# Splitting the first weight loads of a fused feed-forward and linear-attention kernel over three DMA queues

## The chip, the cores and the metric

The kernel runs on one core of one Trainium2 chip. A core has TensorE (matmuls, "PE" in the profile, with "PEld" for the loading of the stationary operand), VectorE ("DVE"), ScalarE ("ACT"), GpSimd ("POOL") and SyncE ("SP"), which only issues DMAs. ScalarE and GpSimd can issue DMAs as well. The metric is the device time of one execution in microseconds (us); lower is better. Of the kernel before, three runs were timed, and one further execution was taken with the hardware profiler.

## The reference

Two branches work on the same input x of 2048 rows by 512 columns, and a gate for each row mixes them:

```
qkv = x @ wqkv                                   # 32 heads of 16
phi(t) = [softmax(t @ w_phi), softmax(-t @ w_phi)]   # per head
o = phi(q) (phi(k)^T v) / (phi(q) (phi(k)^T 1) + 1e-6)
a = o @ wo
b = relu(x @ w1 + b1)^2 @ w2 + b2                # 512 -> 1792 -> 512
g = sigmoid(sum(x * gate_w))                     # one number per row
out = g * a + (1 - g) * b
```

All is float32. The change touches only the first part of branch b: the first product with w1.

## The kernel before

To keep float32 accuracy on TensorE the kernel writes every operand as a high part and a low part of the type fp32r: `hi` is a rounded copy, `lo = src - hi`. A product is then three matmuls, high by high, high by low and low by high. So each piece of data that comes from memory passes through two elementwise operations, one copy (mostly on ScalarE) and one subtraction (on VectorE), before TensorE may use it.

The feed-forward branch cuts the 1792 hidden columns into 14 chunks of 128 (a chunk is called `f` or `fc`) and the 2048 rows into 4 blocks of 512. A hidden chunk of one block, called `u`, is a sum over four slices of 128 of the 512 inputs, numbered k = 0 to 3. The weights of seven chunks are held at a time; the kernel sweeps over the blocks twice. Between these matmuls, a table of slots (`at(slot, step)`) spreads the steps of the attention branch over the time. The order on each engine is that in which the program issues the instructions, apart from those that a scheduler with priorities moves; `tc.issue_after(i)` keeps an instruction behind instruction i on that scheduler's list.

What the change touches is the beginning, `warm_up` and `start`:

- `warm_up` (L457) fills a tile `zeros` on VectorE and lets TensorE do 11 matmuls on it (`idle(11)`, L465), whose results are thrown away.
- `start` (L468) computes the first three chunks (`FIRST = 3`) of block 0 together, slice by slice of the inputs, since then each slice can be used as soon as it is there. For each k it loads `xT[0, :, k, :]` (256 KB, by SyncE's queue, tile `in`) and the weights of the three chunks for this k (192 KB, by ScalarE's queue, tile `row`, L478). It makes `xh`, `xl` from the first and `w1h`, `w1l` from the second, and issues nine matmuls (L501). For k = 0 VectorE makes `w1h` (L488) and ScalarE makes `xh` (L491); for the others ScalarE makes both.
- The order of the nine is: all three chunks' xh·w1h, then all three xl·w1h, then all three xh·w1l. Only for k = 3 they go chunk by chunk, so that the first chunk is finished early and `hidden` (L404) can begin on it: ScalarE applies relu with the bias `b1c`, squares, and the result is split into `hh` and `hl`.
- The fourth chunk's weights (`do_w1(FIRST)`) and the first chunk of w2 go into `row` tiles, too, by SyncE's queue (L104). There are six `row` buffers, and these loads take the last two.
- The bias `b1c` is loaded by GpSimd's queue (L126), between the instructions that GpSimd has at the start anyway: the identity matrix `ident`, the zeroing of `kvb` and the ones in three tiles `vext`.
- `gwb` and `b2b`, copies of the gate weights and of the second bias in all partitions (256 KB each), are loaded by SyncE's queue at the slots 2 and 9 (L704, L705). `gwb` is first used at L257, `b2b` at the end of the first block.

A DMA signals its end on one of a small set of semaphores that the framework hands out in turn, eight for the queues of SyncE and ScalarE together. So the ninth such DMA waits on its engine until the first has landed, the tenth until the second, and so on.

Of the kernel before, what the change touches and what calls it, by code (L numbers as in the profile page):

```python
# [10 lines left out]
AF = mybir.ActivationFunctionType  # L11
# [5 lines left out]
P = 128  # L17
S, D, H, DH, F = 2048, 512, 32, 16, 1792
NK = D // P
# [6 lines left out]
FIRST = 3  # L26
# [9 lines left out]
def tile_gated_mix(ctx: ExitStack, tc: tile.TileContext, xT, xn, wqT, wkT, wphi, wv, wo, w1, b1, w2, b2, gw, out):  # L36
    nc = tc.nc
# [12 lines left out]
    def used(p):  # L50
        banks.remove(p)
        banks.append(p)
# [32 lines left out]
    def load(src, eng=nc.sync):  # L85
        t = stage.tile([P, 512], F32, tag="in", name="in")
        eng.dma_start(t, src)
        return t

    def row():  # L90
        return work.tile([P, D], F32, tag="row", name="row", bufs=6)

    def ffn_tiles(nm, fc):
        return (fpool.tile([P, 512], F32R, tag=nm + "h", name=f"{nm}h{fc}"),
                fpool.tile([P, 512], F32R, tag=nm + "l", name=f"{nm}l{fc}"))

    def by_k(tiles):
        return [tuple(z[:, k * P:(k + 1) * P] for z in tiles) for k in range(NK)]

    def load_ffn(nm, src, fc):  # L100

        if (nm, fc) in (("w1", FIRST), ("w2", 0)):
            t = row()
            nc.sync.dma_start(t, src)  # L104
        else:
            t = load(src)
        hi, lo = ffn_tiles(nm, fc)
        split(t, hi, lo, nc.scalar, nc.vector)
        return hi, lo
# [11 lines left out]
    st, up_w, down_w = {}, {}, {}  # L121
# [1 line left out]
    ident = const.tile([P, P], F32, name="ident")  # L123
    make_identity(nc, ident)
    b1c = const.tile([P, NF], F32, name="b1c")
    nc.gpsimd.dma_start(b1c, b1)  # L126
    gwb = const.tile([P, D], F32, name="gwb")
    b2b = const.tile([P, D], F32, name="b2b")
    gate = const.tile([P, NB * NC], F32, name="gate")
# [36 lines left out]
    def joint_start(loaded):  # L166
        wph, *t = loaded
        two = lambda a: a.rearrange("p (h c) -> p h c", h=2)
        st["W"], st["raw"] = {}, {}
        tmp = work.tile([P, 4 * D], F32, tag="phiT", name="tmp", bufs=1)  # L170
        st["tmp"] = tmp[:, :2 * D], tmp[:, 2 * D:]
        st["slots"] = [work.tile([P, 2 * D], F32R, tag=t, name=f"slot{t}", bufs=1) for t in ("o0", "o1", "ez")]
        for k in (0, 2, 1, 3):
            r = st["tmp"][k // 2] if k % 2 else work.tile([P, 2 * D], F32, tag="e", name=f"raw{k}", bufs=2)
            st["raw"][k] = r
            nc.sync.dma_start(two(r)[:, :, 256:], two(wv[k * P:(k + 1) * P, :]))

    def whole(k):
        wph, *t = st["wT"]
# [224 lines left out]
    def hidden(fc, ps):  # L404
        r = work.tile([P, SB], F32, tag="r", name="r")
        with tc.high_priority(offset=AHEAD):
            st["relu"] = nc.scalar.activation(r, ps, AF.Relu, bias=b1c[:, fc:fc + 1])  # L407
        nc.scalar.activation(r, r, AF.Square)  # L408
        hh = work.tile([P, SB], F32R, tag="hh", name="hh", bufs=LAG + 1)
        hl = work.tile([P, SB], F32R, tag="hl", name="hl", bufs=LAG + 1)  # L410
        st["act"] = split(r, hh, hl, nc.scalar, nc.vector)
        st["dve"] = st["lo"]
        return hh, hl
# [24 lines left out]
    def do_joint(j, piece):  # L438
        if (j, piece) == (0, 0):
            joint_start(st["wT"])  # L440
        with tc.issue_after(st["up"].ins):
            joint(j, piece)
        if (j, piece) == (1, 0):
            banks.remove(ps_b)
# [5 lines left out]
    def do_w1(fc):  # L450
        up_w[fc] = by_k(load_ffn("w1", w1[fc], fc))

    def do_w2(fc):
        down_w[fc] = load_ffn("w2", w2[fc * P:(fc + 1) * P, :], fc)


    def warm_up():  # L457
        z = st["zeros"] = work.tile([P, 512], mybir.dt.bfloat16, tag="r", name="zeros")
        nc.vector.memset(z, 0.0)
        st["warm"] = ps_a.tile([P, 512], F32, tag="s", name="warm")  # L460
        idle(11)

    def idle(n):
        for _ in range(n):
            st["up"] = nc.tensor.matmul(st["warm"], st["zeros"][:, :P], st["zeros"], start=True, stop=True)  # L465


    def start():  # L468
        fs, wide = range(FIRST), FIRST * P
        W = [ffn_tiles("w1", f) for f in fs]  # L470
        ps = [p.tile([P, SB], F32, tag="s", name="u") for p in (ps_e, ps_b, ps_f)]
        xs = st["x", 0] = []
        for f in fs:
            up_w[f] = [tuple(z[:, P * f:P * (f + 1)] for z in W[k]) for k in range(NK - 1)]
            up_w[f].append(tuple(z[:, wide:] for z in W[f]))
        for k in range(NK):
            u, t = load(xT[0, :, k, :]), row()
            nc.scalar.dma_start(t[:, :wide].rearrange("p (f c) -> p f c", f=FIRST),  # L478
                                w1[:FIRST, :, k * P:(k + 1) * P].rearrange("f p c -> p f c"))
            xh, xl = (xpool.tile([P, SB], F32R, tag=g, name=f"{g}0_{k}") for g in ("xh", "xl"))  # L480
            xs.append((xh, xl))
            if k < NK - 1:
                w = [(t[:, :wide], *(z[:, :wide] for z in W[k]))]
            else:
                w = [(t[:, P * f:P * (f + 1)], *(z[:, wide:] for z in W[f])) for f in fs]
            for src, hi, lo in w:
                if k == 0:
                    nc.vector.tensor_copy(hi, src)  # L488
                else:
                    nc.scalar.activation(hi, src, AF.Copy)  # L490
            nc.scalar.activation(xh, u, AF.Copy)  # L491
            low = nc.vector.tensor_tensor(xl, u, xh.bitcast(F32), ALU.subtract)
            with tc.issue_after(low.ins):
                for src, hi, lo in w:
                    nc.vector.tensor_tensor(lo, src, hi.bitcast(F32), ALU.subtract)
            terms = [(f, 0, xh) for f in fs] + [(f, 0, xl) for f in fs] + [(f, 1, xh) for f in fs]
            if k == NK - 1:
                terms.sort(key=lambda x: x[0])
            for f, part_, x in terms:
                with tc.issue_after(st["up"].ins):  # L500
                    st["up"] = nc.tensor.matmul(ps[f], up_w[f][k][part_], x, start=k == 0 and (part_, x) == (0, xh),  # L501
                                                stop=k == NK - 1 and part_ == 1)
        do_w1(FIRST)
        for f in fs:
            hid[f] = hidden(f, ps[f])
            if f == 0:
                st["act0"] = st["act"]
        for p in (ps_e, ps_b, ps_f):
            used(p)
# [191 lines left out]
    def at(slot, f, *a):  # L701
        steps.setdefault(int(2 * slot) / 2, []).append(lambda: f(*a))

    at(2, lambda: nc.sync.dma_start(gwb, gw.partition_broadcast(P)))  # L704
    at(9, lambda: nc.sync.dma_start(b2b, b2.partition_broadcast(P)))  # L705
    for fc in range(LAG + 1, NFH):
        if fc > FIRST:
            at(2 * (fc - LAG) - 2, do_w1_first, fc)
        at(2 * (fc - LAG) - (2 if fc == LAG + 1 else 1), do_w2, fc)
# [50 lines left out]
    hid, last = {}, len(work_list) - 1  # L760
# [5 lines left out]
    def do_up(t, between=lambda: None):  # L766
# [4 lines left out]
        else:  # L771
            between()

    warm_up()
    start()
    with tc.issue_after(st["act0"].ins):
        for fc in range(LAG + 1):
            do_w2(fc)
# [80 lines left out]
```

## Time and profile before

| | |
|---|---|
| runs, us | 513.17, 512.70, 510.85 (median 512.70) |
| the profiled execution, us | 511.04 |
| span of the profile, first to last instruction, us | 509.3 |
| TensorE busy, share of the span | 99% |
| VectorE, ScalarE, GpSimd busy | 79%, 50%, 18% |
| mean granted TensorE clock | 0.999 |

The span is 1.7 us shorter than the execution's time, which also holds what lies before the first and behind the last instruction. The rows of the profile read as follows. A row of the timeline has the start in the span, the time taken (of all instructions that it merges), the engine, the line of the code, the operation and the tiles as output<-input, the count, and in brackets how long the engine was idle before it and what ended this idle time. A letter q behind the engine (SPq, ACTq) marks the issuing of a DMA, which isn't counted as work. A row of the list of groups has the busy time, the mean of one in ns, and the idle time before. A row of the DMA issues has the size, and the median time from the issue to the landing in us. A row of a table by stretches has the stretch, its length, the busy time of PE, PEld, DVE, ACT and POOL with the instructions that began there, the granted clock, the DMA engines' busy share and the GB/s.

### The profile page before, as it was taken

The page shows a single profiled execution, that of the slowest core. Times are in us where ns is not written, and L with a number is a line of the kernel's source. Part 1 is how long each engine was busy: PE and PEld are TensorE (multiplying, and loading weights), DVE is VectorE, ACT ScalarE, POOL GpSimd, SP SyncE. Part 2 cuts the span into 40 slices and gives each one's busy share as a digit, 9 for nine tenths or more (in the row PEclk, how much of TensorE's full clock was granted, in tenths as well). Part 3 has the DMA queues.
Part 4 walks back from the last instruction along what each step waited for, and adds up shares of the span by engine and source line. Part 5 has one row for each costly group of instructions (what it writes and reads, how often), then busy time and mean ns, then how long its engine had stood idle before and what let it go on. Part 6 is the DMA issues. An engine that isn't in the chain of part 4 may idle for free.

```text
span 509.3 us, 9129 instructions
## 1 busy us (share of the span) xinstructions
PE 502.8 (99%) x3421; PEld 408.0 (80%) x3421; DVE 403.5 (79%) x668; ACT 254.8 (50%) x445; POOL 91.0 (18%) x106
## 2 busy tenths in 40 slices
PE   8999999999999999999999999999999999999997
PEld 4888888888788888788888878788787878788775
DVE  3559848888884979796998989897969797897723
ACT  4778645556253565463564744444456354333540
POOL 1001640204320024000012140211222120111200
PEclk9999999999999999999999999999999999999999
DMA  8975696667844478762266131324112231032112
GB/s 256 324 247 186 231 325 194 200 210 226 291 167 142 171 237 288 281 208 83 73 198 228 50 96 40 106 72 143 48 32 85 69 88 47 3 120 68 37 27 83
DMA packets 46628, 76.12 MB, mean 149 GB/s; under 512 B 6776, under 2 KB 23928, under 8 KB 46584
## 3 DMA queue, kind: packets, MB, share of 16 engines
q1 hardware_dynamic: 35544, 41.58, 26.5%
q10 hardware_dynamic: 8224, 24.51, 13.8%
q0 software_dynamic: 2816, 9.45, 5.1%
q8 instruction: 27, 0.44, 0.3%
q14 instruction: 17, 0.14, 0.1%
HBM read 57.68 MB, written 11.54 MB: 136 GB/s over the span
## 4 chain that ended last, share of the span: by engine, by line
PE 93%; DVE 3%; DMA 3%; issue 0%; DVEq 0%; ACT 0%
PE d L77 10%; PE d L78 9%; PE d L79 9%; PE u L77 9%; PE u L78 9%; PE u L79 9%; PE att L79 3%; PE att L78 3%; PE q L78 3%; PE q L77 3%; PE att L77 3%; PE q L79 3%; PE pX L579 3%; PE pX L577 2%; PE pX L578 2%; PE pY L577 2%
## 5 line engine op out<-in xcount | busy, mean ns | idle before, releaser
L407 ACT ACTIVATE r<-u,b1c 128x512 f32<-128x512 f32 x56 | 38.5, 687 | 125.3 <-PE u L79 123.8
L77 PE MATMUL d<-w2h,hh 128*128 128x512 f32 x224 | 87.8, 392 | 0.0
L78 PE MATMUL d<-w2l,hh 128*128 128x512 f32 x224 | 87.3, 390 | 0.0
L79 PE MATMUL d<-w2h,hl 128*128 128x512 f32 x224 | 87.2, 389 | 0.0
L77 PE MATMUL u<-xh,w1h 128*128 128x512 f32 x212 | 83.8, 395 | 0.0
L78 PE MATMUL u<-xl,w1h 128*128 128x512 f32 x212 | 82.6, 390 | 0.0
L79 PE MATMUL u<-xh,w1l 128*128 128x512 f32 x212 | 82.5, 389 | 0.0
L322 POOL TENSOR_TENSOR ez<-e,z 128x512 f32<-128x512 f32 x32 | 42.8, 1358 | 165.9 <-ACT e L294 165.9
L67 DVE TENSOR_TENSOR hl<-r,hh 128x512 fp32r<-128x512 f32 x56 | 37.7, 674 | 23.7 <-ACT hh L64 23.7
L77 PEld LDWEIGHTS d<-w2h,hh 128*128 128x128 f32 x224 | 42.1, 188 | 9.1 <-issue 0.4
L78 PEld LDWEIGHTS d<-w2l,hh 128*128 128x128 f32 x224 | 42.1, 188 | 8.9 <-DVE w2l L67 0.4
L79 PEld LDWEIGHTS d<-w2h,hl 128*128 128x128 f32 x224 | 42.1, 188 | 8.8
L77 PEld LDWEIGHTS u<-xh,w1h 128*128 128x128 f32 x212 | 39.8, 188 | 11.0 <-issue 3.1
L79 PEld LDWEIGHTS u<-xh,w1l 128*128 128x128 f32 x212 | 39.8, 188 | 8.4
L78 PEld LDWEIGHTS u<-xl,w1h 128*128 128x128 f32 x212 | 39.8, 188 | 7.8
L297 DVE TENSOR_REDUCE sm<-e 128x64 f32<-128x1024 f32 x27 | 32.8, 1213 | 11.1 <-ACT e L294 11.1
L294 ACT ACTIVATE e<-e 128x1024 f32<-128x1024 f32 x27 | 28.6, 1059 | 25.0 <-DVE e L292 24.7
L64 ACT ACTIVATE hh<-r 128x512 fp32r<-128x512 f32 x56 | 35.1, 627 | 0.9
L408 ACT ACTIVATE r<-r 128x512 f32<-128x512 f32 x56 | 34.9, 624 | 0.8
L360 ACT ACTIVATE phiT<-tb 32x256 f32<-32x256 f32 x64 | 26.4, 412 | 6.1 <-DVE tb L345 5.1
L329 DVE TENSOR_REDUCE dz<-ez 128x64 f32<-128x1024 f32 x16 | 19.4, 1210 | 11.6 <-POOL ez L322 11.6
L616 ACT ACTIVATE tmp<-pX 128x512 f32<-128x512 f32 x24 | 14.3, 597 | 27.3 <-PE pX L579 27.3
(171 smaller groups left out, 982.2 us busy)
## 6 DMA issues: line engine op xcount, KB each, us to landing
sloto<-wkeep ACTq DMA_DIRECT2D x30, 512.0 KB, 4.2
in<-in_xT SPq DMA_DIRECT2D x44, 256.0 KB, 3.7
slotez<-wkeep ACTq DMA_DIRECT2D x15, 512.0 KB, 4.5
phiT<-tb SPq DMA_DIRECT2D x192, 32.0 KB, 1.9
in<-in_w SPq DMA_DIRECT2D x23, 256.0 KB, 3.3
part<-row POOLq DMA_DIRECT2D x16, 256.0 KB, 5.0
row<-part SPq DMA_DIRECT2D x16, 256.0 KB, 3.1
out<-row SPq DMA_DIRECT2D x15, 256.0 KB, 2.2
```

The lines of the kernel that those rows point to most:

```text
L64: i = nc.scalar.activation(hi, src, AF.Copy)
L67: st["lo"] = elo.tensor_tensor(lo, src, hi.bitcast(F32), ALU.subtract)
L77: nc.tensor.matmul(o, ah[:, sa], bh[:, sb], start=first, stop=False)
L78: nc.tensor.matmul(o, ah[:, sa], bl[:, sb], start=False, stop=False)
L79: return nc.tensor.matmul(o, al[:, sa], bh[:, sb], start=False, stop=last)
L294: nc.scalar.activation(ef, ef, AF.Exp)
L297: nc.vector.tensor_reduce(sm, e3, AX.X, ALU.add)
L322: nc.gpsimd.tensor_tensor(ez[:, hs, :], e3[:, hs, :], zbc[half], ALU.mult)
L360: nc.scalar.activation(dst, src, AF.Copy)
L407: st["relu"] = nc.scalar.activation(r, ps, AF.Relu, bias=b1c[:, fc:fc + 1])
L408: nc.scalar.activation(r, r, AF.Square)
L577: nc.tensor.matmul(ps, h, wh, start=first and j == 0, stop=False, skip_group_check=True)
```

## The change

The four loads of the first weights are distributed anew. ScalarE's queue gets the first chunk's part of k = 0 alone (64 KB), then all of k = 1, then all of k = 3. GpSimd's queue gets the other two chunks' part of k = 0 (128 KB), then all of k = 2. For k = 0, VectorE now copies the rows (`xh`), and ScalarE the weights, in two pieces as they were loaded; the matmuls of k = 0 go chunk by chunk, as those of k = 3 do. For the other k, ScalarE copies the rows first and then the weights. The bias `b1c` moves from GpSimd's queue to SyncE's, behind the four loads of rows; `gwb`, `b2b`, the loads of `wv` and of the w2 chunks are held behind the fourth chunk's load. Two of the 11 matmuls on zeros are dropped.

```
         if (nm, fc) in (("w1", FIRST), ("w2", 0)):
             t = row()
-            nc.sync.dma_start(t, src)
+            st["row"] = nc.sync.dma_start(t, src)
...
     b1c = const.tile([P, NF], F32, name="b1c")
-    nc.gpsimd.dma_start(b1c, b1)
...
-            nc.sync.dma_start(two(r)[:, :, 256:], two(wv[k * P:(k + 1) * P, :]))
+            with tc.issue_after(st["row"].ins):
+                nc.sync.dma_start(two(r)[:, :, 256:], two(wv[k * P:(k + 1) * P, :]))
...
     def do_w2(fc):
-        down_w[fc] = load_ffn("w2", w2[fc * P:(fc + 1) * P, :], fc)
+        with tc.issue_after(st["row"].ins):
+            down_w[fc] = load_ffn("w2", w2[fc * P:(fc + 1) * P, :], fc)
...
-        idle(11)
+        idle(9)
...
+        raw = [(load(xT[0, :, k, :]), row()) for k in range(NK)]
+        for eng, parts in (nc.scalar, ((0, 0, 1), (1, 0, FIRST), (3, 0, FIRST))), (nc.gpsimd, ((0, 1, FIRST), (2, 0, FIRST))):
+            last = None
+            for k, a, b in parts:
+                with tc.issue_after(last.ins) if last else nullcontext():
+                    last = eng.dma_start(raw[k][1][:, a * P:b * P].rearrange("p (f c) -> p f c", f=b - a),
+                                         w1[a:b, :, k * P:(k + 1) * P].rearrange("f p c -> p f c"))
+            if eng is nc.scalar:
+                fetched = last
         for k in range(NK):
-            u, t = load(xT[0, :, k, :]), row()
-            nc.scalar.dma_start(t[:, :wide].rearrange("p (f c) -> p f c", f=FIRST),
-                                w1[:FIRST, :, k * P:(k + 1) * P].rearrange("f p c -> p f c"))
+            u, t = raw[k]
...
-            if k < NK - 1:
+            if k == 0:
+                w = [(t[:, a:b], *(z[:, a:b] for z in W[k])) for a, b in ((0, P), (P, wide))]
+            elif k < NK - 1:
...
-            for src, hi, lo in w:
+            with tc.issue_after(fetched.ins):
                 if k == 0:
-                    nc.vector.tensor_copy(hi, src)
+                    nc.vector.tensor_copy(xh, u)
                 else:
-                    nc.scalar.activation(hi, src, AF.Copy)
-            nc.scalar.activation(xh, u, AF.Copy)
+                    nc.scalar.activation(xh, u, AF.Copy)
+                for src, hi, lo in w:
+                    fetched = nc.scalar.activation(hi, src, AF.Copy)
...
-            if k == NK - 1:
+            if k in (0, NK - 1):
                 terms.sort(key=lambda x: x[0])
...
+        nc.sync.dma_start(b1c, b1)
         do_w1(FIRST)
...
+    def rows_alike(t, src):
+        with tc.issue_after(st["row"].ins):
+            nc.sync.dma_start(t, src.partition_broadcast(P))
+
+    at(2, rows_alike, gwb, gw)
+    at(9, rows_alike, b2b, b2)
```

Three places of the order of instructions are shown. The first is GpSimd's beginning, up to its first DMA of weights; `in_w` and `in_b` are the weights and biases in memory. Before:

```order
masks.py:197 MEMSET ident 128x128
L126 DMA b1c<-in_b 128x14
masks.py:199 ISA
masks.py:199 AFFINE_SELECT ident<-ident 128x128
L132 MEMSET kvb 128x256
L139 MEMSET vext_112 128x32
L139 MEMSET vext_113 128x32
L139 MEMSET vext_114 128x32
```

And with the change:

```order
masks.py:197 MEMSET ident 128x128
L131 MEMSET kvb 128x256
masks.py:199 ISA
masks.py:199 AFFINE_SELECT ident<-ident 128x128
L138 MEMSET vext_111 128x32
L138 MEMSET vext_112 128x32
L138 MEMSET vext_113 128x32
L482 DMA row<-in_w 128x2x128
L482 DMA row<-in_w 128x3x128
```

The bias has left this queue, and the two loads of weights (k = 0's other two chunks, and k = 2) stand behind all seven instructions that GpSimd has there.

The second place is TensorE's first nine matmuls on data, all of k = 0, the number behind `u` telling the chunk. Before, the first seven of them:

```order
L501 MATMUL u_138<-xh0_0_145,w1h0_132 128x512
L501 MATMUL u_139<-xh0_0_145,w1h0_132 128x512
L501 MATMUL u_140<-xh0_0_145,w1h0_132 128x512
L501 MATMUL u_138<-xl0_0_146,w1h0_132 128x512
L501 MATMUL u_139<-xl0_0_146,w1h0_132 128x512
L501 MATMUL u_140<-xl0_0_146,w1h0_132 128x512
L501 MATMUL u_138<-xh0_0_145,w1l0_133 128x512
```

And with the change:

```order
L512 MATMUL u_135<-xh0_0_155,w1h0_129 128x512
L512 MATMUL u_135<-xl0_0_156,w1h0_129 128x512
L512 MATMUL u_135<-xh0_0_155,w1l0_130 128x512
L512 MATMUL u_136<-xh0_0_155,w1h0_129 128x512
L512 MATMUL u_136<-xl0_0_156,w1h0_129 128x512
L512 MATMUL u_136<-xh0_0_155,w1l0_130 128x512
L512 MATMUL u_137<-xh0_0_155,w1h0_129 128x512
L512 MATMUL u_137<-xl0_0_156,w1h0_129 128x512
L512 MATMUL u_137<-xh0_0_155,w1l0_130 128x512
```

The three that need only the first chunk's weights now come first, and the fourth is the first that needs what GpSimd's queue loads.

The third place is SyncE's queue behind the loads of rows, as one piece of the difference (a minus is a row of before, a plus one of the change):

```order
 L87 DMA in<-in_xT 128x512 x4
+L514 DMA b1c<-in_b 128x14
 L104 DMA row<-in_w 128x512 x2
-L704 DMA gwb<-in_gw 128x512
+L87 DMA in<-in_w 128x512
+L786 DMA gwb<-in_gw 128x512
+L145 DMA row<-in_wphi 128x512
 L87 DMA in<-in_w 128x512 x2
-L146 DMA row<-in_wphi 128x512
```

The bias stands in front of the fourth chunk's weights, `gwb` has moved back by one load, and `wphi` forward by two.

More of the change, by code (lines that the diff above doesn't have):

```diff
@@ L702, in at @@
         steps.setdefault(int(2 * slot) / 2, []).append(lambda: f(*a))
-    at(2, lambda: nc.sync.dma_start(gwb, gw.partition_broadcast(P)))
-    at(9, lambda: nc.sync.dma_start(b2b, b2.partition_broadcast(P)))
     for fc in range(LAG + 1, NFH):
```

## The prediction

> **What bounds the kernel now.** I read the page first, then the chain of work that ended last, then the windows, and last the timeline of the first 20 us.
>
> ```profile
> PE 502.8 (99%) x3421; PEld 408.0 (80%) x3421; DVE 403.5 (79%) x668; ACT 254.8 (50%) x445; POOL 91.0 (18%) x106
> PE 93%; DVE 3%; DMA 3%; issue 0%; DVEq 0%; ACT 0%
> 60.00:130.00 70.00, 70.00 (x554) 57.77 (x553) 56.42 (x97) 37.95 (x65) 20.28 (x29) 1.00 0.72 244
> 0.74 5.40 DMA row<-in_w
> 6.16 0.37 DVE w1h L488
> 6.67 8.54 PE u L501 x36
> 15.21 0.23 PE u L77
> 17.93 0.23 PE d L77
> 18.16 0.50 PE d L78
> ```
>
> The first two lines are the page's busy times and the shares of the chain: TensorE is busy for 99% and holds 93% of the chain. The third is the table by stretches for 60 to 130 us, where TensorE works without a gap. The rest is the chain in order of time. So behind the beginning almost nothing but TensorE's own work sets the end, and whatever moves the time at which TensorE has done its first 36 matmuls (L501) moves the end by as much. That time is 15.21. Everything below is about this number. Between 15.21 and 17.93 stand twelve matmuls, 2.72 / 12 = 0.227 us each; 36 of them would be 8.16 us, so that 8.54 holds 0.38 us of waits.
>
> What the first of them waits for is in the timeline:
>
> ```profile
> 1.19 4.87 PE L465 MATMUL warm<-zeros 128*128 128x512 bf16 x11 [1.19 <-DVE zeros L459]
> 4.58 0.15 PEld L465 LDWEIGHTS <-zeros 128*128 128x128 bf16 x1 [0.28 <-issue]
> 5.01 0.15 PEld L465 LDWEIGHTS <-zeros 128*128 128x128 bf16 x1 [0.27 <-issue]
> 5.52 0.63 ACT L491 ACTIVATE xh<-in 128x512 fp32r<-128x512 f32 x1 [1.37 <-DMA in<-in_xT]
> 6.16 0.36 DVE L488 CAST w1h<-row 128x384 fp32r<-128x384 f32 x1 [5.03 <-DMA row<-in_w]
> 6.67 0.93 PE L501 MATMUL u<-xh,w1h 128*128 128x512 f32 x3 [0.60 <-DVE w1h L488]
> ```
>
> The rows of k = 0 have landed by 5.52, where ScalarE starts on them. The weights land at 6.16, 0.64 us later; VectorE copies them in 0.37, and 0.14 after that (6.53 to 6.67) TensorE begins. It has idled since 6.06, the end of the matmuls on zeros. So the weights are late, not the rows, and the most that better weights can bring is bounded by the rows at 5.52.
>
> **The change, part by part.** First the three matmuls that need the first chunk's quarter only.
>
> ```profile
> L488 DVE CAST w1h<-row 128x384 fp32r<-128x384 f32 x1 | 0.4, 359 | 5.0 <-DMA row<-in_w 5.0
> L492 DVE TENSOR_TENSOR xl<-in,xh 128x512 fp32r<-128x512 f32 x4 | 2.8, 690 | 2.0 <-ACT xh L491 2.0
> L495 DVE TENSOR_TENSOR w1l<-row,w1h 128x128 fp32r<-128x128 f32 x3 | 0.7, 284 | 0.0
> L490 ACT ACTIVATE w1h<-row 128x384 fp32r<-128x384 f32 x2 | 1.1, 526 | 2.5 <-DMA row<-in_w 2.5
> L490 ACT ACTIVATE w1h<-row 128x128 fp32r<-128x128 f32 x3 | 0.7, 294 | 0.0
> ```
>
> These are groups with the mean of one in ns. The quarter is a third of the bytes that landed at 6.16, first on its queue, so I take it to be there, and copied in 0.29, before the rows are. VectorE's copy of 512 columns isn't in the trace; it lies between the 0.36 of 384 columns and 0.48 in proportion, and I take 0.45. Then `xh` is there at 5.52 + 0.45 = 5.97 and the first matmul starts at 6.11, against 6.67. But the second needs `xl`: 5.97 + 0.69 + 0.14 = 6.80. The third needs the quarter's `w1l`: 6.66 + 0.28 + 0.14 = 7.08, and ends at 7.31. In the old order all three xh·w1h filled this wait; chunk by chunk they can't. So of 0.56 us of earlier start, TensorE stands at 7.31 with three matmuls done and 33 to go. If nothing waits any more, it is through at 7.31 + 33 x 0.227 = 14.80, **0.41 us earlier** than 15.21. That is the whole gain at hand.
>
> The fourth matmul needs the other two chunks' part of k = 0, which now comes by GpSimd's queue.
>
> ```profile
> 1.31 0.70 POOL L126 DMA_DIRECT2D b1c<-in_b  x1 [0.37 <-issue]
> 2.11 0.30 POOL masks.py:199 TENSOR_SCALAR_AFFINE_SELECT ident<-ident 128x128 f32<-128x128 f32 x1
> 2.34 0.32 POOL L132 MEMSET kvb<- 128x256 f32 x1
> 2.59 0.28 POOL L139 MEMSET vext<- 128x32 f32 x3
> b1c<-in_b POOLq DMA_DIRECT2D x1, 7.0 KB, 6.4
> wkeep<-spare POOLq DMA_DIRECT2D x1, 512.0 KB, 2.9
> q0 software_dynamic: 2, 0.00, 1.0%
> 5.00:5.50 0.50, 0.50 (x3) 0.15 (x1) 0.00 (x0) 0.00 (x0) 0.00 (x0) 1.00 1.07 336
> 5.50:6.00 0.50, 0.50 (x2) 0.00 (x0) 0.00 (x0) 0.48 (x1) 0.00 (x0) 1.00 1.10 371
> ```
>
> GpSimd ended at 2.87, with 0.70 for the bias's DMA and 0.37 of idle time before it. With that gone its work ends near 1.8; with the same 0.37 before a DMA the issue begins at 2.1. The two rows of landing times are the ends for what follows: the bias's 7 KB, the first DMA on this queue, took 6.4 us, the 512 KB of a later one 2.9. The row of q0, GpSimd's queue, is that of the DMA view for 5.0 to 5.5 us: two packets, and none stand in the view of 1.3 to 5.0. So the bias's packets began 3.7 to 4.2 us after its issue at 1.31. The load now is the first on the queue in the same microseconds, so this row is the nearest: packets from 5.8 to 6.3 on. The last two rows have the DMA engines fully busy (1.07, 1.10) at 336 to 371 GB/s; at a third of some 350, 128 KB take 1.1 us. **The landing, T, is then 6.9 to 7.4; I take 7.2.** ScalarE's copy of 256 columns is the mean of its 294 and 526 ns, 0.41, and with 0.14 the fourth matmul starts at 7.75. TensorE is through at 7.75 + 33 x 0.227 = 15.24: +0.03 us. The wait that went (for all weights of k = 0) is replaced by one for two thirds of them, at almost the same place. The two cases meet at T = 7.31 - 0.55 = 6.76; above it each us of T is a us of time, and T = 7.17 is the point of no change.
>
> The ends: with T = 2.1 + 2.9 = 5.0 nothing waits, -0.41. With 2.1 + 6.4 = 8.5 and 1.0 us for the 121 KB more, T = 9.5 and the sum is +2.3.
>
> The other k follow from T. ScalarE goes on with `xh` and `w1h` of k = 1 (0.62 + 0.53) until T + 1.56; TensorE wants them at T + 0.55 + 6 x 0.227 = T + 1.91, so 0.2 us are left. For k = 2 ScalarE ends at T + 2.71 and TensorE arrives at T + 3.95, so GpSimd's second load may land 3.3 us behind the first; it is issued one DMA (0.7) later. k = 3 has moved forward on ScalarE's queue. I cost these at nothing, under cover of TensorE's backlog.
>
> Then SyncE's queue.
>
> ```profile
> in<-in_xT SPq DMA_DIRECT2D x1, 256.0 KB, 7.2
> 7.52 0.33 SPq L704 DMA_DIRECT2D gwb<-in_gw  x1
> 13.89 0.69 ACT L407 ACTIVATE r<-u,b1c 128x512 f32<-128x512 f32 x1 [1.51 <-PE u L501]
> 18.13 0.34 SPq L252 DMA_DIRECT2D row<-in_xn  x1
> L257 DVE SCALAR_TENSOR_TENSOR row<-row,gwb x1: 683/683/683, 29.4 to 29.4; 128x512 f32<-128x512 f32 x1
> ```
>
> The last of the four loads of rows, issued at about 2.2, took 7.2, so the bias behind it on the queue lands at about 9.5 to 10; its first use is at 13.89. `gwb` was issued at 7.52 and is used at 29.4, and so is the first row of `xn`, issued at 18.13, which `b2b` (0.43 us of issuing) now precedes. Over 4 us of cover each: nothing. The four matmuls' later wait of 0.27 us (18.16, 0.50 long) hangs on ScalarE's work behind the first chunk's end and moves with it. Two matmuls on zeros less cost nothing by themselves, as TensorE waits behind them.
>
> **The sum** is +0.03 us on the profiled execution's 511.04: 511.1. The three runs shown have 512.70 as their median, 1.66 above that execution, for a reason that the profile doesn't show; since the prediction is of a median, it is 512.7 + 0.0 = **512.7**.
>
> On spreading loads over queues the Trainium skill speaks against this change ("DMA: Bandwidth & Descriptors", section "Issuing engines are not separate DMA queues"): all queues run on the same 16 engines, and more issuers save only issuing time. The trace agrees where it can: the shares of 1.07 and 1.10 above. By that rule 5.52 for the rows stays as it is, as in my sum.
>
> **The rivals.**
>
> GpSimd's first load is quick, T below 6.76. For it: the 2.9 us row. Against it: the bias. It gives -0.41 at most, 512.3. The same page ("Latency and other measured facts") puts the first byte by GpSimd's path at about 1 us; by it, an estimate, T would be near 4.5 and this rival would hold. The bias's 3.7 us or more contradict it, at least for a queue's first DMA.
>
> GpSimd's first load is as slow as the bias or slower, because its packets, too, come one by one among full engines. From T = 7.17 on the kernel is slower; at T = 8.5 by 1.3, 514.0, at 9.5 by 2.3, 515.0.
>
> The clock is lost. The loads of weights for the matmuls on zeros stand 0.43 us apart up to 5.01 (4.58 to 5.01), against 0.227 later, so TensorE ran at about half speed until somewhere between 5.44 and 6.67, 4.3 to 5.5 us behind its start, although the granted clock reads 1.00. With nine it stops at 1.19 + 9 x 0.43 = 5.06, does three separate matmuls and idles again until 7.75. If the full speed comes only after another 4.3 to 5.5 us of work from there, 10 to 13 matmuls take 0.43 instead of 0.227: +2.0 to +2.6, near 515.0. It decides if the switch hasn't come by 7.75. For it: the switch came only at the end of the eleven. Against it: the idle stretches are about 1 us and less than 0.5. The Trainium skill ("TensorE: Matmul & The Clock Gate", "What's actually happening") has a free-running window of about 3.4 us that must be busy before the clock is raised. By that page, an estimate: the 3.9 us of nine hold such a window for 0.5 us of phases, the 4.9 us of eleven for 1.5, of 3.4 each, and this rival would come often; the trace agrees with a rise after more than 3.4 us, but shows one phase only.
>
> The change does nothing for the start, as the rows of k = 0 land later, with a third queue among them from 5.8 on. 0.3 us of delay gives +0.0 to +0.3, as long as T decides.
>
> **How the numbers follow.** Forecast, T between 6.8 and 8.0, -0.4 to +0.8: 0.47. Quick queue: 0.20. Slow queue: 0.14. Clock: 0.13. Late rows: 0.06. A measurement of this kernel can tell about 0.5%, 2.6 us, from no change. No term reaches -2.6; the runs' own spread of 2.3 us leaves 0.05 for faster. Slower by that much needs the clock's upper end or two rivals together: 0.07. Same: 0.88. For the range, the low end is -0.41 and the 1.66 by which a median can lie at the profiled execution: 510.6; the high end is the slow queue's or the clock's 2.3: 515.0.
>
> **What would show it.** Right: TensorE's first matmul on data near 6.1, the second 0.7 later, a gap before the fourth that ends 0.5 us behind GpSimd's landing, the end of the 36 within 0.8 us of 15.2, and single matmuls 0.227 apart from the first on. A first packet on q0 near 3.4 shows the quick queue; the fourth matmul behind 8.5 the slow one; matmuls 0.43 apart on data the clock. I am wrong altogether if the end of the 36 and the end of the kernel move by different amounts.

## The result, and the profile after

| | before | after |
|---|---|---|
| median of six runs, us | 511.59 (510.85 to 513.17) | 515.26 (514.71 to 517.30) |
| the profiled execution, us | 511.04 | 515.11 |
| span, us | 509.3 | 513.3 |
| mean granted TensorE clock | 0.999 (the profiled execution) | 0.995 (the profiled execution), 0.993 (each of the other five) |
| the 36 first matmuls end at, us | 15.21 | 19.06 |

The changed kernel takes 1.0073 times as long as the one before (95% interval 1.0058 to 1.0089), 3.7 us more by the medians. Three views tell where. First the chain of waits, in order of time (start, time taken, what):

```profile
1.65 7.52 DMA row<-in_w
...
9.19 0.42 ACT w1h L502
...
9.66 9.40 PE u L512 x33
19.06 0.23 PE u L77
```

GpSimd's load of the other two chunks is issued at 1.65, as the chain shows, and lands 7.52 us later, at 9.17. ScalarE's copy of its 256 columns follows, then the 33 matmuls that remain of the first 36. They end at 19.06, which is 3.85 later than before's 15.21; between these two executions the whole span grew by 4.0. So the loss is made in the first 19 us, and almost nothing comes on top. The timeline of TensorE and of the two engines that feed it shows the rows of k = 0, the wait and what follows it:

```profile
4.75 0.43 DVE L498 CAST xh<-in 128x512 fp32r<-128x512 f32 x1 [3.62 <-DMA in<-in_xT]
...
4.92 0.31 ACT L502 ACTIVATE w1h<-row 128x128 fp32r<-128x128 f32 x1 [1.44 <-DMA row<-in_w]
9.19 0.42 ACT L502 ACTIVATE w1h<-row 128x256 fp32r<-128x256 f32 x1 [3.96 <-DMA row<-in_w]
...
5.33 0.76 PE L512 MATMUL u<-xh,w1h 128*128 128x512 f32 x1
5.96 0.80 PE L512 MATMUL u<-xl,w1h 128*128 128x512 f32 x1
6.55 0.50 PE L512 MATMUL u<-xh,w1l 128*128 128x512 f32 x1
9.66 0.50 PE L512 MATMUL u<-xh,w1h 128*128 128x512 f32 x1 [2.61 <-ACT w1h L502]
9.99 0.46 PE L512 MATMUL u<-xl,w1h 128*128 128x512 f32 x1
10.26 0.63 PE L512 MATMUL u<-xh,w1l 128*128 128x512 f32 x1
10.68 0.63 PE L512 MATMUL u<-xh,w1h 128*128 128x512 f32 x1
```

The beginning is quicker than before: the first data matmul starts at 5.33, against 6.67. Then TensorE has nothing for 2.61 us, until ScalarE has copied what GpSimd's queue brought. And when it goes on, its matmuls stand 0.43 us apart from 10.26 on (10.26, 10.68 and so on), not 0.227. The table by stretches gives the clock there; the columns are the busy times of PE, PEld, DVE, ACT and POOL, then the granted clock, the DMA engines' share and GB/s:

```profile
7.00:8.00 1.00, 0.05 (x1) 0.00 (x0) 0.00 (x0) 0.00 (x0) 0.00 (x0) 1.00 1.11 375
...
9.00:10.00 1.00, 0.34 (x2) 0.30 (x2) 0.36 (x1) 0.81 (x2) 0.00 (x0) 1.00 1.03 347
10.00:11.00 1.00, 1.00 (x4) 0.79 (x3) 0.90 (x3) 1.00 (x4) 0.00 (x0) 0.59 1.03 379
11.00:12.00 1.00, 1.00 (x4) 0.71 (x4) 1.00 (x3) 1.00 (x4) 0.00 (x0) 0.50 1.05 348
12.00:13.00 1.00, 1.00 (x4) 0.81 (x3) 1.00 (x3) 1.00 (x4) 0.00 (x0) 0.50 0.94 354
13.00:14.00 1.00, 1.00 (x5) 0.79 (x4) 1.00 (x4) 0.11 (x1) 0.00 (x0) 0.70 0.75 236
```

From 7.05 to 9.19 no engine works while the DMA engines are full (shares of 1.03 to 1.11). Then the clock stands at half for some 3.4 us, 0.41 + 0.50 + 0.50 + 0.30 = 1.71 us of full speed that is missing. That leaves 3.85 - 1.71 = 2.1 us for the wait itself. Two losses, then, of about the same size: a wait, and a clock that goes down after it.

The mean clock of an execution has to be read with care. It also counts a drop behind TensorE's last matmul, which costs nothing: in e2_fill below, the whole of a mean of 0.998 comes from there. So a mean of 0.998 alone shows no loss at the start. One slow stretch of 3.4 us makes 1.71 / 513 = 0.0033. The 0.993 of the other five runs of the change is more than one stretch and such a drop make together; in e8_bias_first (0.992) the clock is at half from 7.3 to 14.1, which begins in the wait. The profiled execution of the change, with one slow stretch, is then not the usual one. The times differ little (514.71 to 517.30 for the five, 515.11 for it).

### The profile page after: what moved, and what is told of

The parts are those of the page before. It is cut to its first block, busy times and chain, and to the rows that moved or that the text cites. A ratio compares the mean times of both kernels' runs of the same rounds, so it can differ in the third digit from the quotient of the medians.

```text
span 513.3 us, 9135 instructions
## 1 busy us (share of the span) xinstructions
PE 504.7 (98%) x3419; PEld 408.9 (80%) x3419; DVE 404.6 (79%) x669; ACT 254.6 (50%) x446; POOL 91.3 (18%) x107
## 4 chain that ended last, share of the span: by engine, by line
PE 84%; DVE 8%; DMA 5%; issue 1%; ACT 1%; POOL 0%; DVEq 0%; ACTq 0%; POOLq 0%
PE d L77 8%; PE d L78 8%; PE d L79 8%; PE u L77 8%; PE u L78 8%; PE u L79 8%; PE att L79 3%; PE att L77 3%; PE q L77 3%; PE att L78 3%; PE q L79 3%; PE q L78 3%; PE pX L589 2%; PE pX L591 2%; PE pX L590 2%; PE kvps L312 2%
```

## The experiments

Three questions were open. Is it the wait that costs, and how much of the 3.7 us is the clock? Is the clock lost through the wait, or through the two matmuls on zeros that were dropped (L462, 11 before, 9 now)? And why does GpSimd's load take 7.5 us? Ratios are to the kernel before, timed on the same chip beside each run, with the 95% interval. Diffs are against the changed kernel, where nothing else is said.

### e1_scalar: no load of weights on GpSimd's queue

```
-        for eng, parts in (nc.scalar, ((0, 0, 1), (1, 0, FIRST), (3, 0, FIRST))), (nc.gpsimd, ((0, 1, FIRST), (2, 0, FIRST))):
+        for eng, parts in (nc.scalar, ((0, 0, 1), (0, 1, FIRST), (1, 0, FIRST), (2, 0, FIRST), (3, 0, FIRST))),:
```

The bias is back on GpSimd's queue, too, as in the kernel before; the order of the matmuls, VectorE's copy of the rows and the nine matmuls on zeros stay.

> The changed kernel with GpSimd's two weight loads given to ScalarE's queue (first chunk's quarter, rest of k = 0, k = 1, k = 2, k = 3) and the bias back on GpSimd's queue. Theory A (the loss is GpSimd's late first load plus the clock window lost in the gap): the rest of k = 0 is there by 6.0 to 6.6 us, no gap of over 0.5 us before TensorE's fourth matmul, the 36 matmuls through by 14.4 to 15.2 us instead of 19.1, the time 510.3 to 511.6, 4 us under the changed kernel. Rival B (the new order of copies and matmuls of k = 0 costs it): the gap goes but the end of the 36 stays above 16, the time 513 or more. Rival C (any third piece of the bytes lands late because the 16 DMA engines are full): the rest of k = 0 lands near 9 on this queue, too, and the time stays near 515.

Measured: 511.61 us against 512.08, ratio 0.9988 (0.9968 to 1.0009). The loss is gone. The chain of the profiled execution, which was one with the clock lost (0.997; one more run has 0.997, one has 0.998, and seven have 1.0):

```profile
0.74 4.78 DMA in<-in_xT
...
6.00 0.70 DVE xl L504
...
6.75 9.84 PE u L513 x35
```

No DMA of weights stands in it any more; the rows of k = 0 set the start, and the second matmul waits for `xl`. The time came out as expected, the end of the 36 (16.59 in this execution) did not, for a reason that is the second question: TensorE had idled from 4.6 to 6.1, and the clock dropped at about 7.3 here, too. So the third queue's load is the cause of the loss; that a gain is left is not shown. The bias moved back in the same edit, but it is not what helps: e8_bias_first moves it back alone and keeps the loss, and e12_none_early leaves it on SyncE's queue and loses nothing like 3.7 us.

### e2_fill: the wait filled with work

```
+                if (k, f, part_) == (0, 1, 0) and x is xh:
+                    for _ in range(12):
+                        with tc.issue_after(st["up"].ins):
+                            idle(1)
```

Twelve more matmuls on zeros stand in front of the fourth data matmul. They compute nothing that is used.

> The changed kernel with 12 more matmuls on zeros between TensorE's third and fourth matmul on data, so that it stays busy while it waits. Theory A: the load of GpSimd's queue still lands at 9.0 to 9.4 us and the fourth matmul starts within 0.3 us of 9.7, but from there on the matmuls stand 0.227 us apart, the 36 are through at 17.1 to 17.5 instead of 19.1, and the time is 1.6 to 2.0 us under the changed kernel, near 513.4. Rival (the clock plays no part, the slow matmuls behind the gap wait for operands): the end of the 36 stays at 19 or moves later, the time stays at 515 or above.

Measured: 514.46, ratio 1.0034 (1.0018 to 1.0051), with a granted clock of 0.998 to 1.0 in all ten runs (in the profiled one, 0.998, it reads 1.00 until TensorE's last matmul is done). The chain:

```profile
6.13 0.73 PE u L516 x2
6.86 2.61 PE warm L466 x12
9.51 7.77 PE u L516 x33
```

The 33 matmuls now take 7.77 us, against 9.40, after a wait that ends at the same place (9.51, against 9.66). So 9.40 - 7.77 = 1.6 us of the loss is the clock's. By the runs it is 1.0073 - 1.0034 = 0.39%, 2.0 us, where the two intervals together allow some 0.8 to 3.2, and what is left for the wait is 0.34%, 1.7 us. The two halves of the loss are separated, and the matmuls on zeros show that the clock answers to TensorE's idling.

### e3_poolfirst: GpSimd's load issued earlier

```
+                with tc.issue_after(last.ins) if last else nullcontext(), tc.high_priority(offset=2000) if eng is nc.gpsimd else nullcontext():
```

The load of k = 0's other two chunks moves ahead of all seven of GpSimd's own instructions, that of k = 2 ahead of three of them.

> The changed kernel with GpSimd's first weight load moved ahead of all its other work (issue near 0.8 us instead of 1.65). If the first DMA of this queue takes a fixed time after its issue (4.8 us to its first packet in the changed kernel, 4.1 in the one before), its first packet comes at 4.9 to 5.6 and the load lands at 7.9 to 8.5, about 0.9 earlier than 9.2, and the fourth matmul moves with it. If the queue only starts at a certain time, or when the DMA engines have room, the first packet stays at 6.3 to 6.5 and the landing at 9.2.

Measured, one run: 513.34 us, clock 0.995. The chain:

```profile
1.27 7.05 DMA row<-in_w
...
8.35 0.42 ACT w1h L502
...
8.81 9.12 PE u L512 x33
```

Issued 0.38 earlier (1.27; 0.8 had been expected), the load lands 0.85 earlier, and the 36 end 1.13 earlier (8.81 + 9.12 = 17.93). Its first packet stands in the view of 5.6 to 5.7, 4.3 to 4.4 us behind the issue, so it moved with the issue. The time follows the landing, and the order on GpSimd is not what makes it late.

### e4_hidden: GpSimd's queue only for k = 2 and k = 3

```
+        for eng, parts in (nc.scalar, ((0, 0, 1), (0, 1, FIRST), (1, 0, FIRST))), (nc.gpsimd, ((2, 0, FIRST), (3, 0, FIRST))):
```

> The changed kernel with the rest of k = 0 and k = 1 on ScalarE's queue, and k = 2 and k = 3 on GpSimd's. Theory A: GpSimd's queue is as late as before (its first load lands near 9.2 to 9.6), but k = 2 is wanted only near 9.8 and k = 3 near 12, so the lateness is hidden: the 36 matmuls are through by 14.5 to 15.4 and the time is 510.3 to 511.8, as with all on ScalarE's queue. Rival C (a third queue slows all loads): the 36 end above 16 and the time is above 512.5.

Measured: 512.61, ratio 1.0007 (0.9988 to 1.0026), clock 0.999 to 1.0 in all runs. The chain still holds GpSimd's load, and the timeline has the first matmul behind the 36 at 15.01:

```profile
1.67 6.44 DMA row<-in_w
8.13 0.53 ACT w1h L502
...
8.71 5.11 PE u L512 x21
```

```profile
15.01 0.39 PE L77 MATMUL u<-xh,w1h 128*128 128x512 f32 x1
```

The load takes 6.4 us here, too, but TensorE has other work for most of that time. The same row of the kernel before is

```profile
15.05 0.39 PE L77 MATMUL u<-xh,w1h 128*128 128x512 f32 x1
```

so the 36 end as early as before. (The timeline shows a matmul's start before the one ahead of it has ended; the 15.21 of the chain is this same place, 0.16 later.) The median is 0.8 us above the upper end that was expected, but the interval of its ratio includes 1. A slow queue alone costs little; a slow queue in front of the fourth matmul costs the wait.

### e5_before9, e6_scalar11, e7_scalar13: the matmuls on zeros

The first is the kernel before with `idle(9)` for `idle(11)`; the other two are e1_scalar with 11 and with 13.

> The kernel before with 9 matmuls on zeros in place of 11, nothing else. If the two matmuls fewer are by themselves enough to lose the clock, most runs show a mean granted clock of 0.997 or less and the time is 1 to 2 us above the kernel before. If the loss in the changed kernel comes from the long wait before the fourth matmul (2.6 us there, 1.6 us of idle time here before the first), a minority of runs lose it and the median is within 0.6 us of the kernel before.

> The run with all weights on ScalarE's queue, with 11 matmuls on zeros again. The trace of that run had the clock fall from 7.3 to 10.7 us, after 1.5 us of idle time before the first matmul on data, and the 36 matmuls through at 16.6. With 11 the idle time is 0.2 to 0.6 us: the clock should stay up, the 36 be through by 14.4 to 15.0 us, and the median be 0.3 to 0.8 us under the kernel before. If the clock had nothing to do with it, the 36 end at 16 or later again.

> The same with 13 matmuls on zeros, which end near 6.3 to 6.8 us, behind the landing of the first rows and weights: no idle time, no loss of the clock in any run, but the first matmul on data up to 0.6 us later than with 11. Forecast: within 0.4 us of the run with 11, with less spread between runs.

Measured: 1.0010 (0.9995 to 1.0025), 1.0000 (0.9983 to 1.0017) and 0.9998 (0.9984 to 1.0013). With nine, the kernel before has a clock of 0.997 in one run of ten, and of 0.998 to 1.0 in the others; e6 and e7 have 0.999 or 1.0 in all. The chain of e7_scalar13 shows the start with the clock kept:

```profile
5.64 0.44 DVE xh L499
...
6.85 8.39 PE u L513 x35
```

35 matmuls take 8.39, against 9.84 in the execution of e1_scalar. So two matmuls on zeros less bring the clock to the edge, but they don't lose 3.7 us by themselves. e6_scalar11 keeps the clock as expected, but not the rest: its 36 end at 15.40, not by 15.0, and no gain shows. And the end of the 36 in e7_scalar13, 15.24, is that of before: with five loads on ScalarE's queue and the bias on GpSimd's, the rows land late again (5.64), and the earlier start is eaten by `xl`.

### e8_bias_first: is only the first DMA on GpSimd's queue slow?

```
+    nc.gpsimd.dma_start(b1c, b1)
...
-        nc.sync.dma_start(b1c, b1)
```

> The changed kernel with the bias back on GpSimd's queue at its old place, ahead of the two weight loads (which are then issued near 3.0 us instead of 1.65). If only the first DMA of this queue is slow to start, the bias pays for it (first packet near 5.0 to 5.6) and the weights' packets follow within 1 us of it, although they are issued 1.3 us later: landing at 8 to 9. If each DMA that GpSimd issues in these microseconds takes 4 to 4.8 us from its issue to its first packet, the weights' packets start above 7 and land above 9.8.

Measured, one run: 515.39 us, clock 0.992. The chain, and GpSimd's row of the DMA view for 7.2 to 7.4 us, the first with packets of the weights:

```profile
2.78 6.47 DMA row<-in_w
9.27 0.42 ACT w1h L503
...
9.74 9.81 PE u L513 x33
```

```profile
q0 software_dynamic: 5, 0.02, 27.5%
```

The weights are the second DMA on the queue, issued at 2.78, and they still take 6.47 us. The two theories disagree here. The landing at 9.25 lies between them, a little nearer to "only the first is slow" (8 to 9, against above 9.8). The packets, which the theories are about, began at 7.2 to 7.4, 4.4 to 4.6 us after their issue, as for a queue that is slow each time (above 7). A cost that only a queue's first DMA pays does not explain it.

### e9_after11: the changed kernel with eleven matmuls on zeros

The only edit is `idle(11)` in place of `idle(9)`.

> The changed kernel with the 11 warm-up matmuls of before in place of its 9. If the wait of TensorE for GpSimd's load (6.55 to 9.66 us) is what loses the clock afterwards, two more matmuls ahead of the first data matmul change nothing: the fourth data matmul still starts at 9.4 to 9.9, the matmuls from about 10 on stand 0.43 us apart again for some 3 us, the granted clock is at most 0.996 in all runs, and the ratio to before is 1.005 to 1.009. If the two dropped warm-up matmuls are what loses it, the clock stays at 0.998 or more, and the ratio falls to the share of the wait alone, 1.002 to 1.005.

Measured: ratio 1.0073 (1.0050 to 1.0096), as without them. But the four runs differ, and the expectation that all would lose the clock missed: 515.37, 516.30 and 514.87 us with clocks of 0.993, 0.993 and 0.997, and the profiled one, 513.45 with 1.0. That execution's timeline of TensorE:

```profile
9.57 0.50 PE L512 MATMUL u<-xh,w1h 128*128 128x512 f32 x1 [2.83 <-ACT w1h L502]
...
10.38 0.39 PE L512 MATMUL u<-xh,w1h 128*128 128x512 f32 x1
10.60 0.39 PE L512 MATMUL u<-xl,w1h 128*128 128x512 f32 x1
```

The same wait, even a little longer (2.83), and matmuls 0.22 to 0.23 apart behind it. So the wait puts the clock at stake, and something that differs from run to run decides; e2_fill, with the wait filled, lost it in none of ten. The Trainium skill ("TensorE: Matmul & The Clock Gate", "What's actually happening") describes a free-running window of about 3.4 us over which activity is judged. The trace agrees in the length of the slow stretch (about 3.4 us in the table above) and in that one kernel goes both ways. The section "Why this matters for your kernels" of that page of the Trainium skill names idle gaps of more than about 3 us as those to avoid. The runs differ: a gap of 2.61 was enough in the profiled execution of the change, and one of 1.5 in that of e1_scalar.

### e10_two_only: the version that might beat both

```
+        for eng, parts in ((nc.scalar, ((0, 0, FIRST), (1, 0, FIRST), (3, 0, FIRST))), (nc.gpsimd, ((2, 0, FIRST),))):
```

With `idle(11)`.

> Only the third chunk's load (k=2) goes to GpSimd's queue; ScalarE's takes k=0 whole (not in two pieces), k=1 and k=3; 11 warm-up matmuls. If the end of the first 36 matmuls carries through to the end of the kernel, as the theory of a late load has it: first rows land at 4.6 to 5.0 as in the other kernels with three loads on ScalarE's queue, GpSimd's load at 8 to 9.2, before its matmuls need it (from about 9.5), the 36 are through by 14.6 to 15.3 against 15.21 before, and the ratio is 0.998 to 1.000. If what is gained at the start is given back behind it (the rival: the other order of SyncE's loads makes a stall later, as in the kernel with k=2 and k=3 on GpSimd's queue), the 36 are through as early and the ratio is 1.000 to 1.002.

Measured: 511.43 against 511.79, ratio 0.9995 (0.9981 to 1.0008), clock 0.998 to 1.0. The chain, and then the times at which one kind of matmul (`pX` of `sloto` and `xh`) first and last starts, for this kernel and for the one before:

```profile
6.07 8.61 PE u L512 x36
14.67 0.23 PE u L77
```

```profile
L589 PE MATMUL pX<-sloto,xh x16: 389/389/389, 54.2 to 217.3; 128*128 128x512 f32 x16
```

```profile
L577 PE MATMUL pX<-sloto,xh x16: 388/389/390, 54.3 to 217.1; 128*128 128x512 f32 x16
```

The 36 end at 14.67, 0.54 earlier than before, as expected. At 54 us 0.1 is left of it (54.2 against 54.3). In e12_none_early and e4_hidden, where the 36 end 0.29 and 0.04 earlier than before, the same matmul first starts at 54.8 and 55.0; in the change, where they end 3.85 later, at 58.2, which is 3.9 later. So an earlier end of the 36 is gone by 54 us in these executions, while a later one stays. The 0.2 that the kernel is behind at 217 us (217.3 against 217.1) says nothing: from the first to the last of these matmuls, the profiled executions take from 162.2 to 164.1 us. What takes the gain back wasn't settled, and with these intervals a version that beats the one before isn't shown.

### e11_alone and e12_none_early: why GpSimd's load is slow

In e11_alone GpSimd's queue gets one more load, of 128 KB, ahead of the others, and SyncE's and ScalarE's first loads are held until it has landed:

```
+        lone = stage.tile([P, 512], F32, tag="in", name="in")
+        nc.gpsimd.dma_start(lone[:, :2 * P].rearrange("p (f c) -> p f c", f=2), w1[1:FIRST, :, :P].rearrange("f p c -> p f c"))
+        seen = const.tile([P, 1], F32, name="seen")
+        fetched = nc.scalar.activation(seen, lone[:, :1], AF.Copy)
+        held = nc.sync.dma_start(lone, xT[0, :, 0, :])
```

In e12_none_early all first weights go over ScalarE's queue as in e1_scalar, the bias stays on SyncE's, and there are 11 matmuls on zeros. GpSimd's first DMA of the program is then a store at 32 us.

> The changed kernel with a further load of 128 KB as GpSimd's first DMA, and the first loads of SyncE and ScalarE held until it has landed, so that GpSimd's first DMA finds the DMA engines empty. The kernel's time is no question here (the whole start moves by the landing, 4 to 7 us). If the full DMA engines of the start delay a first DMA on GpSimd's queue, its packets begin 1.0 to 1.6 us after its issue, as those of 31 us on do, and 128 KB land within 3 us of it. If the delay is the queue's own at the start of a program, whatever else runs, the packets begin 3.2 to 4.9 us after the issue, and it lands 4.5 us or more after it.

> All weights on ScalarE's queue (k=0 in two pieces, then k=1, 2, 3), the bias on SyncE's as in the changed kernel, 11 warm-up matmuls: GpSimd issues no DMA before its first store at about 31 us. If a queue's first DMA is slow as such, that store's packets begin 3 us or more after its issue. If the start's microseconds make it slow, they begin 1.0 to 1.6 us after it, as in the kernels where it is the second or third DMA on the queue. The 36 first matmuls end at 15.2 to 15.6 with the clock kept, or about 16.6 without it; the time is 0.997 to 1.003 of before's.

Measured, one run each: 516.62 and 512.17 us, against one run of the kernel before with 511.60. The chain of e11_alone, and GpSimd's row of its DMA view for 3.2 to 3.7 us (packets, MB, share); its view for 1.5 to 3.2 has no packet at all:

```profile
1.65 2.83 DMA in<-in_w
```

```profile
q0 software_dynamic: 31, 0.10, 71.8%
```

The DMA is the first on its queue, as large and issued in the same microsecond as the one of the change, and lands after 2.83 us in place of 7.52. Its packets begin 1.6 to 2.1 us after the issue. In the change, the view for 1.5 to 6.4 us has none of this queue, and that for 6.4 to 6.9 these:

```profile
q1 hardware_dynamic: 46, 0.08, 46.3%
q10 hardware_dynamic: 134, 0.07, 43.6%
q0 software_dynamic: 9, 0.04, 17.9%
```

So they begin 4.8 to 5.3 us after the issue, and at first get 18% of the engines while SyncE's q1 and ScalarE's q10 hold 90. Over the whole time up to the landing, 6.4 to 9.2, it is a third:

```profile
q0 software_dynamic: 109, 0.32, 34.0%
```

But the 0.32 MB are those of both of GpSimd's loads. The 192 KB of k = 2, issued at 2.52, went through in the same microseconds as the 128 KB. In e12_none_early the queue's first DMA is issued at 32.00, and its first packets stand in the view of 33.8 to 34.3, 1.8 to 2.3 us behind it, when the other queues are less busy:

```profile
q0 software_dynamic: 29, 0.12, 57.6%
q1 hardware_dynamic: 29, 0.06, 34.0%
```

The delay belongs to the other queues' traffic at the start, not to a first use: this pair shows it, with one execution each. A first use may still cost some tenths, since the 1.8 us or more lie above the 1.0 to 1.6 that were expected. Nor is the engines' share alone what counts: q1 holds 67% of them from 31 to 33.8 in e12_none_early, q1 and q10 together 81% from 1.5 to 6.4 in the change. The Trainium skill ("DMA: Bandwidth & Descriptors", "Anatomy of one DMA — SWDGE (gpsimd) path") gives 2.0 us and the bytes at 436 GB/s for such a DMA, an estimate of 2.3 us for 128 KB. The empty engines' 2.83 is near it; the full engines' 7.52 is not. Through which step the traffic holds the queue back no run here shows. The other queues are not quick at the start either. In e12_none_early the same 128 KB stand on ScalarE's queue, behind the quarter, and its chain has

```profile
1.18 5.36 DMA row<-in_w
```

Issued 0.47 earlier and 2.16 quicker, they land at 6.54, 2.63 before the change's 9.17.

The start of e12_none_early, from its timeline, shows what the change would have brought without the wait:

```profile
5.51 0.68 PE L512 MATMUL u<-xh,w1h 128*128 128x512 f32 x1
...
7.03 0.50 PE L512 MATMUL u<-xh,w1h 128*128 128x512 f32 x1 [0.18 <-ACT w1h L502]
...
14.76 0.39 PE L77 MATMUL u<-xh,w1h 128*128 128x512 f32 x1
```

The first data matmul starts at 5.51, the fourth at 7.03, and the first one behind the 36 at 14.76, against 15.05 in before's timeline: 0.29 earlier, and earlier than expected. It is not seen in the time of this run, 512.17.

## Why the prediction was wrong, point by point

**The frame held.** The end of the 36 was named as the one number that matters, with the loss carried through one for one: 3.85 there, 4.0 in the span. For gains it doesn't hold (e10_two_only: 0.54 earlier, 0.1 left at 54 us), which the prediction did not see.

**The three matmuls of the quarter.** Their mutual distance was right: VectorE's copy took 0.43 (0.45 foreseen), the second matmul came 0.63 behind the first (0.69). All of it lay 0.8 earlier than forecast, 5.33 instead of 6.11, since the rows landed at 4.75 and not at the 5.52 that was kept from before. It helped nothing, as what came next was the wait. By the rule of the Trainium skill that the prediction cites ("DMA: Bandwidth & Descriptors", "Issuing engines are not separate DMA queues") the prediction kept 5.52; the measured 4.75 differs. The third queue is not the reason, since e12_none_early, with no load on it, has 4.90.

**The step that failed is T**, the landing of GpSimd's first load: 6.9 to 7.4 foreseen, 9.17 measured. The formula around it was right: T + 0.55 for the fourth matmul gives 9.72 (measured 9.66), and T = 9.17 gives +2.0 for the end, against the 2.1 that the wait cost. T was mis-sized in two ways. First, its packets began at 6.4 to 6.9, not 5.8 to 6.3, although the issue came at 1.65, earlier than the 2.1 foreseen. Second, and more, the 128 KB were given 1.1 us from the first packet, at a third of the engines' rate; they took 2.3 to 2.8. The queue did get its third, 34% from 6.4 to 9.2, but two loads shared it, 320 KB in place of 128, where the sum gave the third to the first load alone. Whether the first would have landed sooner without the second was not tried; in e10_two_only 192 KB alone on this queue took 7.9 us from issue to landing. The quoted rows had the warning in them: the bias, 7 KB on the same queue in the same microseconds, took 6.4 us from issue to landing. With a load of 128 KB issued at 2.1, that made 8.5 the likely least. The prediction took that row apart into a first packet and a transfer, and put it as an outer end where it was the nearest whole measurement. e11_alone shows why that row applied: the slowness goes with the traffic, and that is the same in both kernels. The rival named for it ("one by one among full engines", T of 8.5 to 9.5, +1.3 to +2.3) is the one that came true in T and in the wait's price; it had a chance of 0.14. Its reason, packets one by one, is not what the views show.

**The clock** was a rival of its own, with 0.13 and +2.0 to +2.6, to be decided by whether the switch had come by 7.75. That was the wrong point. In the profiled execution the full speed had come by the fourth matmul: it and the next two start 0.33 and 0.27 us apart (9.66, 9.99, 10.26), and only then do they stand 0.43 apart. (The granted clock alone would not show it, since it reads 1.00 in the slow first microseconds as well.) e2_fill, with the same nine matmuls on zeros ahead and the wait filled, does its twelve at 2.61 / 12 = 0.22 us each and keeps the clock. So it is lost through the wait, not through a switch that comes late: the size was about right (1.6 to 2.0) and the cause wrong. The worst of it is that the two rivals were priced as exclusive, and the range ended at the larger of the two, 515.0. A wait long enough to make one true makes the other likely: 2.1 + 1.7 = 3.8.

**What was cost at nothing** was nothing: k = 1 to 3 followed without a wait once T had come (33 matmuls in 7.77 us where the clock is kept, 7.49 without any gap), and neither the bias nor the gate weights on SyncE's queue appear in the chain.

**The median.** 1.66 us of the forecast level rested on three runs of before with a median of 512.70; six have 511.59. The ratio is free of that. The 512.7 thus lay nearer to the measured 515.26 by luck: the change itself was forecast at 0.0 and measured at +3.7 us.

## What to carry to other kernels

A load that the next matmul needs does not belong on GpSimd's queue at a start at which other queues fill the DMA engines: 128 KB took 7.5 us there, 5.4 on ScalarE's queue among like traffic, and 2.8 on GpSimd's queue with the engines empty. Price a new load by the whole time from issue to landing of the nearest load on the same queue in the same microseconds, and treat the time of a smaller one as the least that a larger one takes (at this start, 7 KB took 5.6 to 6.4 us on GpSimd's queue, 128 KB 6.5 to 7.5, 192 KB 6.4 to 7.9). When a wait of over a microsecond falls on TensorE in a kernel that is bound by it, add the loss of the clock behind it to the price (1.6 to 2.0 us here), since both often come together, though not in every run.

## What the runs showed of the hardware that was not expected

- The clock can drop after idle times well below 3 us, and not always. A wait of 2.6 to 2.8 us (as profiled) went with a lower clock in all six runs of the change (0.993 to 0.995) and in three of the four of e9_after11 (0.993 to 0.997); about 1.5 us without work lost it in the profiled run of e1_scalar, and one more of its ten has the same 0.997. e5_before9 kept it in its profiled run, over an idle time of 1.66 us. What decides stays open.
- The rows of k = 0, the same first DMA of SyncE's queue in every kernel but e11_alone, start to be used at 4.58 to 4.99 in eight of the kernels (4.75 in the change, 4.90 in e12_none_early) and at 5.15 to 5.89 in five (5.52 before, 5.89 in e6_scalar11). The late ones all have the bias on GpSimd's queue and four or five loads on ScalarE's; with five loads but no bias (e12_none_early, 4.90) or the bias but three loads (e8_bias_first, 4.99) they are early. Why the two together delay them wasn't tried.
